# Strassen loop from token 1536, attention at every place of the plain blocks, spectral mixing with one step less

## The chip, the cores and the metric

The kernel runs on one core of a Trainium2 chip. The metric is the time of one execution on the device in microseconds (us), the median of several runs. The engines are called PE (TensorE, the matrix multiplier) with its weight loads (PEld), DVE (VectorE), ACT (ScalarE), POOL (GpSimd) and SP (SyncE, which issues nearly all DMAs here). Each engine executes its own instructions in order and waits for the others by semaphores.

## What is computed

Pooled attention, then two token and channel mixers in a row, on 8 batches of 576 tokens with 512 channels:

```python
# attention: 8 heads of 64; keys and values are means over 8 tokens (72 of them)
scores = scale * np.matmul(q, k_p.transpose(0, 1, 3, 2))
attn = softmax(scores);  x = attn @ v_p            # -> (8, 576, 512)
# first mixer
h = x.transpose(0, 2, 1) @ U @ V                   # rank 32, along the tokens
u = x + h.transpose(0, 2, 1)
x1 = u + np.maximum(u @ w_ch1, 0.0) @ w_ch2        # 512 -> 2048 -> 512
# second mixer
u = x1 + real(fft(fft(x1, axis=1), axis=2))        # spectral mixing
un = layernorm(u)
out = u + np.maximum(un @ w_ch1b, 0.0) @ w_ch2b
```

Numbers are 32 bits wide. The kernel splits a factor into a high and a low part where it needs the precision, so one product becomes three matmuls (high x high, high x low, low x high).

## The kernel before

The 4608 tokens go through the first mixer's channel layers in two ways. The **plain loop** takes the first `2 * SB` pieces of 256 tokens: first pieces 0 and 1 together (g0 below), then one piece at a time (the narrow blocks, g1 and on). A piece has 16 places `f`; at each stands 12 matmuls of 256 columns (`h<-utx,w`) and six of 512 columns (`o<-w,hh`, `o<-w,hl`). Its input is turned by DVE (`block_prep`). The **Strassen loop** takes all further work in blocks of 512 tokens: the rest of the first mixer, then all nine blocks of the second (k0 and on). A block has eight rounds; a round has seven products of six matmuls of 256 columns (`h<-x,wr`) with 24 matmuls of 512 columns between them. Its input is turned by PE: 16 transposes a block (`h<-ident,ul`, or `s<-ident,ul` in the second mixer). Its combined weights come from DRAM (`wc`) through a ring of four tiles (`wr`), 512 KB each, 28 in a block.

Beside these loops run **lanes**, Python generators that are advanced step by step: `a` (attention of a batch, tile by tile), `prep` (means of keys and values), `mix` (the rank 32 mixing), `p` (input of the next block), `w` (weights: `w_combine` makes the Strassen weights of the first mixer from the loaded ones, then `w_second` loads words of `w1b`, converts and combines them and stores them in `wc`, then quarter by quarter `w2b` into `wd`), and `d` (the spectral mixing of a batch, class `Dft`, with its loads `F` and `R` of `x1d` and their sum `S`). `w_combine` has 48 steps, the words of `w1b` 104 and the quarters of `w2b` 66. Weights in work lie in `wo`, a tile with four buffers.

In the plain loop a lane steps once at each place `f`, the weight lane twice at three places of four. In the Strassen loop a function `tick(i)` is called four times in a round with a row of lane names for each `i`; the attention lane steps a fifth time in a round. The lane `d` starts when all others but `p` are done. Batches from `LB` on use another form of the attention step: their rank 32 sum goes through bank `s1` and is added on DVE (`hus`), so that they can run in either loop.

Who sets the order: in the Strassen loop the instructions of PE, DVE and ACT stand as written; in the plain loop ACT's do from g1 on, while a scheduler places those of PE and DVE; on SP and POOL it places them everywhere. SP's queue is in order too: an issue that waits holds all issues behind it.

The places of the program that the change touches: the constants `SB` and `LB` (the first lines of the diff), `Dft.run` (its `yield`s, each of which ends a step), the condition ahead of `step("a")` in the plain loop, and the first row of names in `tick`.

Of the kernel before, what the change touches and what calls it, by code (L numbers as in the profile page):

```python
# [34 lines left out]
NPR = NF // 2  # L35
TA = 512
NBA = NTOK // TA
SB = 4
LB = 6
NOP = 12  # L40
NRING = 4
QAHEAD = 2
# [4 lines left out]
def kernel(  # L47
# [31 lines left out]
    state = {"n": 0, "free": False, "m": "s1", "u": 0, "slot": 0, "x1": 0, "u2": 0, "op": 0, "clock": 0, "flush": False, "lean": False, "four": False, "busy": False, "late": None, "tick": 0, "banks": ("s0", "s1", "hu")}  # L79
# [534 lines left out]
    class Dft:  # L614
# [18 lines left out]
        def run(self, b, group):  # L633
            p1 = self.p
            z = b * S
            slot = b - group[0]
# [26 lines left out]
            yield  # L663
            yield
            yield
            yield
            X, XE = [], []
            for i in range(3):
                f, r, n = fr
                s = tl("S")  # L670
                e = tl("E")
                add(nc.vector, s[:n], f[:n], r[:n])
                yield
                sub(nc.vector, r[:n], f[:n], r[:n])
                nc.gpsimd.tensor_copy(e[:n, 0:1], s[:n, 0:1])
                nc.gpsimd.memset(e[:n, 511:512], 0.0)
                sub(nc.vector, e[:n, 256:511], r[:n, 1:256], r[:n, 256:511])
                add(nc.vector, e[:n, 1:256], s[:n, 1:256], s[:n, 256:511])
                c2 = s[:n, 511:512].to_broadcast([n, 64])
                if i < 2:  # L680
                    fr = loads(i + 1)
                yield
                xe = tl(f"xe{i}", (128, 96 if i < 2 else 64), F32R)
                if i < 2:
                    xh, xl = tl(f"xh{i}", dt=F32R), tl(f"xl{i}", dt=F32R)
                    split(xh, xl, e)
                    nc.scalar.activation(out=xe[:, 0:64], in_=c2, func=ACTF.Copy)
                    sub(nc.vector, xe[:, 64:96], c2[:, 0:32], xe[:, 0:32].bitcast(F32))
                    X.append((xh, xl))
                    XE.append(xe)  # L690
                else:
                    m = self.sm
                    for h, y, w in ((xe, c2, 64), (None, e, 512)):
                        h = h or tl("S", dt=F32R)
                        q = r[:, 0:w]
                        nc.vector.tensor_scalar(out=q[:n], in0=y[:n], scalar1=m[:n, 0:1], scalar2=None, op0=ALU.mult)  # L696
                        nc.scalar.activation(out=h[:n], in_=y[:n], func=ACTF.Copy)  # L697
                        nc.vector.scalar_tensor_tensor(out=h[:n], in0=h[:n].bitcast(F32), scalar=m[:n, 1:2], in1=q[:n], op0=ALU.mult, op1=ALU.add)  # L698
                    X.append((h,))
                    XE.append(xe)  # L700
                yield
                if i < 2:
                    yield
                    yield
            P = []
            if slot == 0:
# [51 lines left out]
            for i in range(n2):  # L758
# [11 lines left out]
                a, bb = bank("s0"), bank("s1")  # L770
# [80 lines left out]
    pools = [mp]  # L851
    seq = [(0, b) for b in range(SB, NBA)] + [(1, b) for b in range(NBA)]

# [373 lines left out]

    groups = [[0, 1]] + [[j] for j in range(2, 2 * SB)]
    late = []
    slot = 0  # L1230
    order = ExitStack()
    for gi, js in enumerate(groups):
        if gi == 1:
            order.enter_context(tc.manual_schedule(engines={mybir.EngineType.Activation}))
        wide = len(js) > 1
        last = js[-1] == 2 * SB - 1
        tags = (("o0", "o1"), ("h1", "m"))
        for f in range(NF):
            state["slot"] = NF * gi + f
            clock()  # L1240
            while (1, min(f + 2, NF - 1)) not in W:
                step("w")
            one = wide or late or f % 2 == 0
            hs = st1(js, f, "h0" if one else "h1")
            if last and f >= NOP:
                ring_load(f - NOP)
            if late and f == 4:
                finish(late.pop())
                state["m"] = "m"
            if f == 0:  # L1250
                begun, rested = False, False
            if not begun and f >= (6 if gi == 1 or last else 1):
                if last:
                    ok = lambda: state["u"] >= (SB + 1) * TA
                else:
                    nj = groups[gi + 1][0]
                    ok = lambda: state["u"] >= (nj + 1) * T
                if f >= (NF - 1 if wide else 9):
                    until(ok)
                if ok():  # L1260
                    begun = True
                    lanes["p"] = prep_a(0) if last else block_prep(nj)
            if not df:
                if gi and "w" not in lanes and len(second) < 2:
                    lanes["w"] = (w_combine, w_second)[len(second)](at)
                    second.append(1)
                spectral()
            prev = hq.pop(0) if len(hq) >= (2 if gi > 1 or (gi == 1 and f > 0) else 1) else None
            for i in range(2 if wide else 1):
                slot += 1  # L1270
                if wide or slot % 4 or state["four"] or gi > 4:
                    step("a")
                step("d")
                if prev and i < len(prev[0]):
                    st2(prev[0][i], prev[1], prev[2][i], tags[i])
                for name in ("p", "mix", "w", "prep", "w") if f % 4 else ("p", "mix", "w", "prep"):
                    step(name)
                if last:
                    step("p")
                    step("p")  # L1280
            if prev and not wide and len(prev[0]) > 1:
                st2(prev[0][1], prev[1], prev[2][1], tags[1])
            if prev and prev[1] == NF - 1:
                finish(prev[0][0])
                if len(prev[0]) > 1:
                    late.append(prev[0][1])
                    rest(prev[0][1])
                else:
                    later(lambda j=prev[0][0]: state.update(x1=(j + 1) * T))
            hq.append((js, f, hs))  # L1290
            if f == NF - 1:
                until(lambda: "p" not in lanes, ["p"] if last else None)
            if not rested and f > 11 and begun and "p" not in lanes:
                rested = True
                rest(js[0])
# [5 lines left out]
    clock()  # L1301
    state["x1"] = SB * TA
    state["banks"] = ("s0",)
# [19 lines left out]
    def tick(i):  # L1323
        state["tick"] = i
        clock()
        swap()
        spectral()
        for name in (("d", "p", "a", "mix", "w"), ("d", "p", "a", "w", "mix", "w"), ("d", "p", "a", "prep", "mix", "w"), ("d", "a", "mix", "p"))[i]:
            step(name)

    def ready_for(k):
# [171 lines left out]
```

## Time and profile before

| | |
|---|---|
| median of 3 runs | 1903.48 us (1902.91 to 1907.74) |
| the profiled execution | 1906.44 us, span of its instructions 1904.6 us |
| PE, PEld busy | 1823.2 us (96%), 1635.6 us (86%) |
| DVE, ACT, POOL busy | 1067.6 us (56%), 717.0 us (38%), 194.3 us (10%) |
| mean granted clock of PE | 0.987 of full speed |
| DMA | 423.78 MB, mean 222 GB/s |
| plain loop, both pieces together (g0) | 71.9 to 201.1 us of the span |
| plain loop, six narrow blocks (g1 to g6) | 201.1 to 582.4 us |
| Strassen loop, 14 blocks (k0 to k13) | 582.4 to 1904.6 us |

Busy time is the union of an engine's instructions; the end of a matmul is modelled, so a small hole between matmuls can be covered. How long work on PE takes is therefore read better from the distance between the starts of consecutive matmuls. The stage limits are the starts of the first matmul of g0, of g1 and of k0. In rows of waits, `A <- B` means that engine A stood idle until B's result came.

### The profile page before, as it was taken

How to read it: one execution, taken by the hardware profiler on the slowest of the kernel's cores; microseconds unless marked ns; L12 is line 12 of the kernel's file. 1: busy time of each engine (PE TensorE's matmuls, PEld its weight loads, DVE VectorE, ACT ScalarE, POOL GpSimd, SP SyncE). 2: the span in 40 equal slices, each digit the busy share in tenths (PEclk: the TensorE clock that was granted, in tenths of full speed). 3: DMA queues.
4: the chain of work that ended last, by engine and by line, in shares of the span. 5: the costliest groups of instructions: out<-in, count | busy, mean ns of one | idle time of the engine just before them, and what ended most of it. 6: DMA issues, size and time to landing. Idle time of an engine off the chain costs nothing. (4 is left out here: it accounts for less than half of the span.)

```text
span 1904.6 us, 31941 instructions
## 1 busy us (share of the span) xinstructions
PE 1823.2 (96%) x11500; PEld 1635.6 (86%) x11500; DVE 1067.6 (56%) x2445; ACT 717.0 (38%) x2198; POOL 194.3 (10%) x340
## 2 busy tenths in 40 slices
PE   5689899999999999999999999999999999999999
PEld 4569788888888888899889898989998999999998
DVE  7894475656565665545465746564656544444332
ACT  5552444444454543333233432333333323233221
POOL 3340131212210000000000000000000000000000
PEclk9799999999999999999999999999999999999999
DMA  9653465857478787867677857685768575756564
GB/s 359 226 186 119 140 198 165 254 175 242 155 249 292 254 280 264 279 211 263 205 246 242 300 185 236 209 278 190 244 214 261 191 234 190 227 182 228 187 206 133
DMA packets 262974, 423.78 MB, mean 222 GB/s; under 512 B 45536, under 2 KB 72256, under 8 KB 262816
## 3 DMA queue, kind: packets, MB, share of 16 engines
q1 hardware_dynamic: 261888, 418.33, 67.2%
q0 software_dynamic: 928, 3.40, 0.5%
q8 instruction: 91, 1.49, 0.3%
q14 instruction: 67, 0.55, 0.1%
HBM read 342.09 MB, written 79.56 MB: 221 GB/s over the span
## 5 line engine op out<-in xcount | busy, mean ns | idle before, releaser
L119 PE MATMUL h<-x,wr 128*128 128x256 f32 x4704 | 642.4, 284 | 6.3 <-DMA wr<-wc 2.8
L119 PEld LDWEIGHTS h<-x,wr 128*128 128x128 f32 x4704 | 616.6, 191 | 37.0 <-DVE side L112 4.1
L119 PE MATMUL o<-w,hh 128*128 128x512 f32 x1312 | 371.4, 399 | 2.9 <-ACT hh L1036 1.6
L119 PEld LDWEIGHTS o<-w,hh 128*128 128x128 f32 x1312 | 229.3, 190 | 39.1 <-ACT hh L1036 4.8
L119 PE MATMUL h<-utx,w 128*128 128x256 f32 x1536 | 214.8, 288 | 17.4 <-DVE hl L1037 10.0
L119 PEld LDWEIGHTS h<-utx,w 128*128 128x128 f32 x1536 | 202.4, 193 | 30.4 <-DVE hl L1037 14.7
L119 PE MATMUL o<-w,hl 128*128 128x512 f32 x656 | 213.7, 396 | 2.3 <-DVE hl L1037 2.3
L112 DVE TENSOR_TENSOR side<-h,side 128x256 f32<-128x256 f32 x224 | 123.9, 553 | 153.4 <-PE h L119 152.6
L1314 ACT ACTIVATE hh<-side 128x256 fp32r<-128x256 f32 x224 | 116.8, 522 | 137.1 <-DVE side L112 129.9
L1314 ACT ACTIVATE hh<-h 128x256 fp32r<-128x256 f32 x112 | 43.1, 385 | 301.3 <-PE h L119 299.6
L1320 DVE SCALAR_TENSOR_TENSOR hl<-h,hh 128x256 fp32r<-128x256 f32 x112 | 47.4, 424 | 186.9 <-ACT hh L1314 186.9
L119 PEld LDWEIGHTS o<-w,hl 128*128 128x128 f32 x656 | 120.2, 189 | 25.2 <-DVE hl L1037 2.9
L1320 DVE SCALAR_TENSOR_TENSOR hl<-side,hh 128x256 fp32r<-128x256 f32 x224 | 123.4, 551 | 28.6 <-ACT hh L1314 28.5
L119 PE MATMUL m<-w,hh 128*128 128x512 f32 x464 | 127.8, 395 | 0.0
L119 PE MATMUL hu<-w,hh 128*128 128x512 f32 x448 | 122.2, 394 | 0.0
L510 ACT ACTIVATE s<-s,mx 128x72 f32<-128x72 f32 x296 | 90.2, 329 | 50.0 <-DVE mx L503 48.9
L109 POOL TENSOR_TENSOR wo<-wo 128x256 fp32r<-128x256 f32 x88 | 67.6, 784 | 302.6 <-ACT wo L115 253.2
L109 DVE TENSOR_TENSOR x<-ul,x 128x256 fp32r<-128x256 f32 x182 | 70.1, 421 | 41.8 <-ACT x L115 41.6
L119 PEld LDWEIGHTS m<-w,hh 128*128 128x128 f32 x464 | 80.4, 190 | 10.8
L119 PEld LDWEIGHTS hu<-w,hh 128*128 128x128 f32 x448 | 77.0, 190 | 10.1
L1361 ACT ACTIVATE side<-h 128x256 f32<-128x256 f32 x112 | 42.8, 382 | 107.3 <-PE h L119 107.2
L119 PE MATMUL m<-w,hl 128*128 128x512 f32 x232 | 72.6, 391 | 0.0
(253 smaller groups left out, 2362.5 us busy)
## 6 DMA issues: line engine op xcount, KB each, us to landing
wr<-wc SPq DMA_DIRECT2D x392, 512.0 KB
wc<-wo SPq DMA_DIRECT2D x88, 256.0 KB
x<-x SPq DMA_DIRECT2D x56, 256.0 KB
ur<-ud SPq DMA_DIRECT2D x36, 256.0 KB
x1d<-ur SPq DMA_DIRECT2D x36, 256.0 KB
ul<-u2d SPq DMA_DIRECT2D x36, 256.0 KB
ur<-u2d SPq DMA_DIRECT2D x36, 256.0 KB
out<-ur SPq DMA_DIRECT2D x36, 256.0 KB
```

Of the source, the lines that this page charges most:

```text
L109: eng.tensor_tensor(out=o, in0=a, in1=b, op=ALU.subtract)
L112: eng.tensor_tensor(out=o, in0=a, in1=b, op=ALU.add)
L119: nc.tensor.matmul(o, a, b, start=start, stop=stop, skip_group_check=True)
L510: nc.scalar.activation(out=s[:n, a], in_=v[:, k], func=ACTF.Exp, bias=mx[:n, a:a + 1], accum_out=sm[:n, a:a + 1])
L1314: nc.scalar.activation(out=hh[:, i], in_=c, func=ACTF.Relu)
L1320: nc.vector.scalar_tensor_tensor(out=hl[:, i], in0=c, scalar=0.0, in1=hh[:, i].bitcast(F32), op0=ALU.max, op1=ALU.subtract)
L1361: nc.scalar.activation(out=sb, in_=v, func=ACTF.Copy)
```

## The change

`SB` falls from 4 to 3: the plain loop ends at token 1536 instead of 2048, with pieces 0 and 1 and four narrow blocks, and the Strassen loop has 15 blocks, six of the first mixer. `LB` falls from 6 to 5. In the plain loop the attention lane now steps at each place of every narrow block; before, it left out every fourth place in blocks 1 to 4. The weight lane steps twice in `tick(0)` of the Strassen loop instead of once. In `Dft.run` two `yield`s go: one between a batch's first loads and their use, and one between the second or third loads and theirs.

```diff
-SB = 4
-LB = 6
+SB = 3
+LB = 5
...
             fr = loads(0)
             yield
             yield
             yield
-            yield
             X, XE = [], []
             for i in range(3):
                 f, r, n = fr
...
                 yield
                 if i < 2:
-                    yield
                     yield
...
             for i in range(2 if wide else 1):
                 slot += 1
-                if wide or slot % 4 or state["four"] or gi > 4:
+                if wide or slot % 4 or state["four"] or gi:
                     step("a")
                 step("d")
...
-        for name in (("d", "p", "a", "mix", "w"), ("d", "p", "a", "w", "mix", "w"), ("d", "p", "a", "prep", "mix", "w"), ("d", "a", "mix", "p"))[i]:
+        for name in (("d", "p", "a", "w", "mix", "w"), ("d", "p", "a", "w", "mix", "w"), ("d", "p", "a", "prep", "mix", "w"), ("d", "a", "mix", "p"))[i]:
             step(name)
```

The order of instructions shows what moves. Three places follow; `hst`, `xh`, `xl` and `ust` belong to the rank 32 mixing, `v,e` to attention times V, `wr` and `x_...` to a Strassen product.

On PE, a tile of attention of batch 6 stands before in the last narrow block, between the matmuls of the plain loop:

```order
L119 MATMUL o_5687<-w,hh 128x512 x2
L119 MATMUL o_5691<-w,hh 128x512 x2
L119 MATMUL s_6310<-xh,ust 128x512
L119 MATMUL s_6310<-xl,ust 128x512
L119 MATMUL h_6339<-utx,w 128x256 x11
L119 MATMUL s_6314<-v,e 128x128
L119 MATMUL s_6314<-v,e 128x192 x3
L119 MATMUL s_6314<-v,e 128x64
L119 MATMUL h_6339<-utx,w 128x256
```

Now all five tiles of this batch stand behind the start of the Strassen loop; on PE one of them reads:

```order
L119 MATMUL h_5099<-x_4659,wr 128x256 x6
L119 MATMUL hu<-w,hh 128x512 x4
L119 MATMUL hu<-w,hl 128x512 x2
L119 MATMUL s_5957<-xh,ust 128x512
L119 MATMUL s_5957<-xl,ust 128x512
L119 MATMUL s_5961<-v,e 128x128
L119 MATMUL s_5961<-v,e 128x192 x3
L119 MATMUL s_5961<-v,e 128x64
L119 MATMUL h_5934<-x_4866,wr 128x256 x6
```

The tile's matmuls are the same; they moved from between plain matmuls to between a round's products. Behind the start of the Strassen loop there are 12 tiles' attention times V where there were eight.

On DVE, the words of `w1b` (L150, L155 and L156 convert one word) stand before in the plain loop, between the `hl<-h` of its places:

```order
L503 TENSOR_REDUCE mx<-s_5732 128x4
L109 TENSOR_TENSOR wo<-wo 128x256
L150 TENSOR_SCALAR wo<-cv 128x256
L418 TENSOR_REDUCE kp<-raw 128x72
L155 SCALAR_TENSOR_TENSOR wo<-cv,wo 128x256
L1037 SCALAR_TENSOR_TENSOR hl<-h_5714,hh 128x256
```

The last 11 of the 32 words now stand in the Strassen loop, between its sums (`side`) and `hl`:

```order
L156 SCALAR_TENSOR_TENSOR wo<-cv,wo 128x256
L109 TENSOR_TENSOR wo<-wo 128x256
L112 TENSOR_TENSOR hus<-s_5326,hus 128x512
L150 TENSOR_SCALAR wo<-cv 128x256
L155 SCALAR_TENSOR_TENSOR wo<-cv,wo 128x256
L156 SCALAR_TENSOR_TENSOR wo<-cv,wo 128x256
L112 TENSOR_TENSOR side<-h_5099,side 128x256
L109 TENSOR_TENSOR hst<-hus,hst 32x512
```

Behind them moved all 32 quarters of `w2b`, of which 24 stood in the Strassen loop before.

On DVE in the spectral mixing, the sum `S<-F,R` of a batch's tail (99 rows) stands before behind two `hl` rounds after the splits `xl`, `xe` of the part ahead of it:

```order
L109 TENSOR_TENSOR xl_9717<-E,xh_9716 128x512
L109 TENSOR_TENSOR xe_9715<-S,xe_9715 128x32
L112 TENSOR_TENSOR side<-h_6400,side 128x256
L112 TENSOR_TENSOR ur<-o_8823,ur 128x512
L1320 SCALAR_TENSOR_TENSOR hl<-h_6400,hh 128x256
L1320 SCALAR_TENSOR_TENSOR hl<-side,hh 128x256
L112 TENSOR_TENSOR side<-h_9645,side 128x512
L112 TENSOR_TENSOR ur<-o_8851,ur 128x512
L1320 SCALAR_TENSOR_TENSOR hl<-side,hh 128x512
L112 TENSOR_TENSOR S<-F,R 99x512
```

Now, on DVE at the same place, it comes after one `side`:

```order
L109 TENSOR_TENSOR xl_9831<-E,xh_9830 128x512
L109 TENSOR_TENSOR xe_9829<-S,xe_9829 128x32
L109 TENSOR_TENSOR x_9836<-ul,x_9836 128x2x128
L109 TENSOR_TENSOR x_9839<-ul,x_9839 128x2x128
L112 TENSOR_TENSOR side<-h_5099,side 128x256
L112 TENSOR_TENSOR S<-F,R 99x512
```

The sum moved ahead of three `hl` rows and a `side`, a step closer to the loads of `F` and `R`, which are issued where the part ahead of it is summed.

## Rows read from the trace of the kernel before

**Rows 1.** Windows by stage: start and end, length, busy PE, PEld, DVE, ACT, POOL, clock, DMA.

```profile
core 0 of [0], span 1904.6 us
...
201.10:582.40 381.30, 362.60 (x2307) 323.58 (x2308) 234.66 (x549) 172.75 (x675) 77.33 (x108) 0.99 0.64 201
582.40:785.50 203.10, 197.84 (x1254) 177.82 (x1253) 115.86 (x270) 86.84 (x292) 5.14 (x12) 0.99 0.83 280
```

**Rows 2.** Timeline of PE in a clean Strassen stretch: start, length, instruction.

```profile
1247.27 1.59 PE L119 MATMUL h<-x,wr 128*128 128x256 f32 x12
1248.71 1.09 PE L119 MATMUL m<-w,hh 128*128 128x512 f32 x4
...
1250.09 1.59 PE L119 MATMUL h<-x,wr 128*128 128x256 f32 x12
```

**Rows 3.** The same timeline in the first Strassen block, with attention.

```profile
600.10 1.14 PE L119 MATMUL s<-k,q 128*128 128x144 f32 x8
600.99 1.69 PE L119 MATMUL h<-x,wr 128*128 128x256 f32 x12
...
610.27 1.53 PE L119 MATMUL s<-v,e 128*128 128x128 f32 x10
611.60 1.68 PE L119 MATMUL h<-x,wr 128*128 128x256 f32 x12
...
620.61 0.66 PE L933 MATMUL h<-ident,ul 128*128 128x128 f32 x4
621.02 0.96 PE L119 MATMUL h<-x,wr 128*128 128x256 f32 x6
```

**Rows 4.** PE's groups in 201.1 to 582.4 us: count, busy, mean ns, idle before.

```profile
L119 PE MATMUL h<-utx,w 128*128 128x256 f32 x1152 | 164.0, 287 | 11.3 <-DVE hl L1037 10.0 <-ACT utx L115 1.0
L119 PE MATMUL o<-w,hh 128*128 128x512 f32 x380 | 115.2, 404 | 2.5 <-ACT hh L1036 1.2 <-DVE ur L112 0.6 <-ACT wo L115 0.6
L119 PE MATMUL o<-w,hl 128*128 128x512 f32 x190 | 68.6, 405 | 0.0
L119 PE MATMUL s<-v,e 128*128 128x192 f32 (+2 forms) x220 | 34.1, 300 | 0.0
L119 PE MATMUL s<-k,q 128*128 128x144 f32 x176 | 29.3, 292 | 0.6 <-DVE x L539 0.5
L516 PE MATMUL s<-ident,s 128*128 128x128 f32 x88 | 18.8, 280 | 3.0 <-ACT s L510 3.0
```

**Rows 5.** DVE's waits in 201.1 to 582.4 us: total us, times, longest.

```profile
DVE wo L109 <- DMA wc<-wo: 14.8, 14, 1.9
...
DVE cv L150 <- DMA wo<-w2b: 6.8, 4, 4.7
...
DVE wo L150 <- DMA cv<-w1b: 3.3, 2, 1.7
```

**Rows 6.** DVE's waits in 582.4 to 785.5 us, the first row.

```profile
DVE hl L1320 <- ACT hh L1314: 36.0, 21, 2.8
```

**Rows 7.** PE's waits in 582.4 to 785.5 us, the first row.

```profile
PE h L119 <- DMA wr<-wc: 2.0, 1, 2.0
```

**Rows 8.** Timelines of SP, DVE and PE at the first, fourth, fifth and last tail.

```profile
803.78 0.27 SPq L656 DMA_DIRECT2D R<-x1d  x1
...
806.92 0.68 DVE L112 TENSOR_TENSOR S<-F,R 99x512 f32<-99x512 f32 x1
...
1091.80 0.40 PE L119 MATMUL s<-st,S 99*128 99x290 f32 x1 [1.16 <-DVE S L698]
...
1184.73 0.21 SPq L656 DMA_DIRECT2D R<-x1d  x1
...
1186.39 0.69 DVE L112 TENSOR_TENSOR S<-F,R 99x512 f32<-99x512 f32 x1 [0.83 <-DMA R<-x1d]
...
1453.40 0.27 SPq L656 DMA_DIRECT2D R<-x1d  x1
...
1461.63 0.68 DVE L112 TENSOR_TENSOR S<-F,R 99x512 f32<-99x512 f32 x1
```

## The prediction

> **What bounds the kernel now.** I read the windows by stage first. The span is 1904.6 us. The first two Strassen blocks hold TensorE busy for 197.8 of 203.1 us, the six narrow plain blocks for 362.6 of 381.3 us [rows 1]. So TensorE's own work sets the time, and what can be won beside it lies in the holes of the plain stage, which are twice as dense (4.9% against 2.6%). Busy time hides part of those holes, because a matmul's end is modelled, so I counted the work itself.
>
> The second view is the timeline of TensorE in a clean Strassen stretch: twelve matmuls of 256 columns take 1.44 us (1247.27 to 1248.71), 0.120 us each, and six of 512 columns take 1.38 us (to 1250.09), 0.230 us each [rows 2]. The third is the same view where attention runs: eight score matmuls 0.89 us, ten of attention times V 1.33 us, four transposes 0.41 us [rows 3]. The fourth is the table of TensorE's groups in the six narrow plain blocks, which gives the counts [rows 4]. Their work is 1152 x 0.120 = 138.2; 634 matmuls of 512 columns (380 and 190 in the rows, and 64 in rows left out: two for each of 22 attention tiles and 20 of the mixing) x 0.230 = 145.8; 220 x 0.133 = 29.3; 176 x 0.111 = 19.6; 125 transposes (88 in the row, 37 left out) x 0.1025 = 12.8. That is 345.7 us of work in 381.3 us: **35.6 us lost, 5.9 us in each narrow block**, nearly twice the idle time of 18.7 us that the window shows.
>
> The fifth view says who is late: the waits of VectorE in that stretch. Nine of its rows name a DMA, 79.7 us in all; most of it is `wo` tiles that wait for their stores (40.8 us in three of the nine), and one wait of 4.7 us is for a `w2b` load [rows 5]. VectorE executes in order, so `hl` stands behind such a wait, and TensorE waits for `hl` (10.0 us on the first group of [rows 4]). In the first two Strassen blocks, where attention and the weight lane run too, the longest row of the same view is `hl` waiting for ScalarE, and none of its ten rows names a DMA [rows 6]. There TensorE is idle 5.3 of 203.1 us [rows 1]; by the plain stage's ratio (35.6 to 18.7) I call that 10 us lost.
>
> **The change part by part.**
>
> *One block of 512 tokens goes from the plain loop to the Strassen loop.* Two narrow blocks issue 2 x 16 x 12 = 384 matmuls of 256 columns; a Strassen block issues 8 x 7 x 6 = 336; the 192 of 512 columns stay. So 48 x 0.120 = 5.76 us of TensorE go. But the plain blocks turn their input on VectorE, a Strassen block on TensorE: 16 transposes x 0.1025 = 1.64 us come. Together **-4.1 us**, and this part stands on the path, since TensorE is the bound before and after. One block more of weights from DRAM (28 ring loads of 512 KB) lies beside it: the first two Strassen blocks ran at a DMA share of 0.83 [rows 1].
>
> *Four narrow blocks stay of six.* At 5.9 us each they lose 23.7 us in place of 35.6. Against that, attention now steps at each of 16 places in a block, where blocks 1 to 4 of before skipped every fourth, so its waits come closer together; I take 26 us. Bounds: 10 us (four blocks at the rate of the first two Strassen blocks, 10 us for 1024 tokens) and 35.6 us (nothing gained). **-9.6 us.**
>
> *What moves into the Strassen loop.* By the order, 12 attention tiles stand behind its start where 8 stood, all 32 quarter loads of `w2b` where 24 stood, and 11 words of `w1b` where there was none. The weight lane steps five times in a product round, not four. Three blocks carry lanes, not two. The longest wait of TensorE in those two blocks is 2.0 us for a weight ring load [rows 7], 3.8 us by the same ratio, and comes once. The other 6.2 us are at most 3.1 us for a further block and at least nothing; I take 1.1, since a part of them belongs to the entry into the loop, which comes once as well. The moved words bring their `wo` waits along: the plain blocks of after take 4 x 28 of the 152 steps that use `wo` so, 40 are left, and 40/152 of 40.8 us are 11 us of VectorE waits. At the plain stage's exchange (35.6 of 79.7) they cost 4.8 us, and nothing if the Strassen order covers them: between the sum that frees a half bank and the next product in it lie one product and six matmuls, 0.72 + 1.38 = 2.1 us [rows 2]. I take half, 2.4. **+3.5 us**, bounds 1 and 6.
>
> *Spectral mixing with a step less.* A step is a quarter of a round of 7 products and 24 matmuls of 512 columns, (5.04 + 5.52)/4 = 2.64 us. Loads of `F` and `R` are used a step sooner. From the issue of the last load of a batch's tail to its sum on VectorE there were 2.9, 2.8, 1.9, 3.7, 1.5, 8.0, 3.8 and 8.0 us in the eight batches (first, fifth and last in [rows 8]). In the fifth VectorE waited 0.83 us, so a load takes 2.28 us from issue to use. With 2.64 us less, six of the eight come late, by 2.1, 2.2, 3.0, 1.2, 3.5 and 1.2 us, 13.1 us of VectorE waits. The Trainium skill, "DMA: Bandwidth & Descriptors", section "Anatomy of one DMA", speaks against this edit: a DMA has a fixed cost of about 2 us, most of it the receipt of the last byte, whatever its size. [...] What reaches TensorE is less: each wait has the 2.1 us of cover above, and the tail's matmul stands three steps behind. I take **+2 us**, bounds 0 and 13.1.
>
> **Sum.** -4.1 - 9.6 + 3.5 + 2.0 = -8.2 us: a span of 1896.4 us. The profiled run took 1906.44 us, 2.96 above the median of 1903.48 us; against the median it is 1903.48 - 8.2 = **1895.3 us**. This kernel's runs can tell about 0.3%, 5.7 us, from no change, so faster means under 1897.8 and slower over 1909.2.
>
> **The rivals.** (A) The forecast, 1890 to 1900 us.
>
> (B) The holes move with the lanes. They come from weight steps and loads, and these are all still done; then the second and third part cancel, and 1903.5 - 4.1 + 2.0 = 1901.4 us. For it: the `wo` waits are half of VectorE's DMA waits and follow the weight lane. Against it: no DMA wait at all on VectorE in the first two Strassen blocks.
>
> (C) Slower: the spectral sums wait for their loads. If TensorE paid the whole step at each of eight tails, 8 x 2.64 = 21.1 in place of 2.0, the time would be 1903.5 - 10.2 + 21.1 = 1914.4 us. For it: the tail's matmul already waited 1.16 us for VectorE in the fourth batch [rows 8], so some chains have no slack. It decides from 2.0 us per batch ((10.2 + 5.7)/8). Against it: five of the eight tails would come at most 2.1 us late, which the cover takes.
>
> (D) More is won: the remaining plain blocks lose half of what they did, 2.95 us each, since the `w2b` wait and a part of the `wo` waits are no longer theirs, and the Strassen loop covers what it takes over: 11.8 - 35.6 = -23.8, and 1903.5 - 4.1 - 23.8 + 1 = 1876.6 us; half way from A, 1886 us.
>
> That the change does nothing can't be: the order shows the block moved.
>
> **How the numbers follow.** A 0.56, B 0.23, C 0.12, D 0.09. A lies under 1897.8 for seven parts in ten (0.40); D is faster whole; of B a tenth is, and the rest is the same; C is slower. So faster 0.52, same 0.36, slower 0.12. The range 1885 to 1906 holds A, B and a part of D and leaves out C.
>
> **What would show it.** Right: the narrow blocks (now four) still take 60 to 65 us each; the blocks with lanes in the Strassen loop, now three, have few VectorE rows that name a DMA; 5040 matmuls of 256 columns on the ring where there were 4704, and 1152 on `utx`; in the spectral stretch VectorE rows S waiting for R of 1 to 3 us at some tails, with TensorE idle under 1 us there. Wrong: TensorE idle in the first three Strassen blocks of over 10 us with the ring or `hl` as the releaser, narrow blocks over 68 us, or a spectral stretch with several idle microseconds a batch.

## The result, and the profile after

The changed kernel takes **1927.82 us** (median of 4 runs, 1926.81 to 1929.37), the kernel before 1904.85 us on the same chip (4 runs, 1902.91 to 1907.74): a ratio of 1.012, interval 1.0103 to 1.0138. It is 23 us slower, where 8.2 us less were forecast. The profiled execution took 1927.33 us with a span of 1925.5 us, 20.9 us longer than before.

The counts came out as forecast. Two groups of the page's table (busy time, mean ns, idle before):

```profile
L119 PE MATMUL h<-x,wr 128*128 128x256 f32 x5040 | 692.1, 285 | 18.5 <-DVE side L112 10.4
L119 PE MATMUL h<-utx,w 128*128 128x256 f32 x1152 | 156.8, 287 | 10.0 <-DVE utx L109 3.9
```

So the time went into waits. The windows, cut as in [rows 1] (the four narrow blocks one by one, then k0, k1, k2, k3 to k9, the rest):

```profile
199.80:268.80 69.00, 63.19 (x399) 54.96 (x399) 39.31 (x90) 29.92 (x124) 14.97 (x21) 1.00 0.57 179
268.80:337.50 68.70, 64.94 (x409) 56.68 (x408) 42.35 (x96) 29.51 (x123) 16.10 (x22) 1.00 0.56 175
337.50:406.90 69.40, 65.57 (x411) 56.85 (x410) 40.38 (x94) 30.51 (x130) 14.03 (x19) 1.00 0.65 204
406.90:467.00 60.10, 59.42 (x394) 54.09 (x393) 46.79 (x114) 35.73 (x137) 12.11 (x16) 1.00 0.80 266
...
467.00:596.20 129.20, 113.68 (x701) 101.81 (x700) 75.94 (x170) 62.58 (x223) 19.83 (x29) 0.95 0.80 267
596.20:695.50 99.30, 97.36 (x612) 86.62 (x610) 60.84 (x145) 44.57 (x146) 3.85 (x7) 1.00 0.88 301
695.50:794.10 98.60, 97.35 (x614) 87.33 (x614) 56.62 (x132) 39.25 (x121) 0.00 (x0) 1.00 0.78 259
794.10:1485.10 691.00, 676.49 (x4321) 612.35 (x4320) 389.68 (x929) 232.10 (x586) 45.22 (x145) 0.99 0.72 234
1485.10:1925.50 440.40, 436.69 (x2742) 393.38 (x2740) 184.04 (x437) 126.57 (x316) 10.28 (x16) 1.00 0.64 202
```

One block stands out: k0, 129.2 us long, TensorE busy for 113.7 of them at a granted clock of 0.95. No other block is near it.

As in the prediction I count what a block **loses**: its length less its matmuls at their prices from start to start, here instruction by instruction. In k0 the products and their 512-column matmuls make 80.5 us, attention 22.5, mixing and transposes 2.9, together 105.9, so it loses 23.4 us (with the block limits unrounded). By this count the six narrow blocks of before lost 32.9 us (35.6 by the group prices of the prediction). All losses below are counted so, each from one profiled execution.

| lost, us | before | after |
|---|---|---|
| narrow blocks | 32.9 (six) | 26.3 (four: 9.7, 7.7, 7.8, 1.2) |
| Strassen blocks with attention and weights | 9.2 (k0 4.5, k1 4.7) | 29.8 (k0 23.4, k1 4.1, k2 2.3) |
| spectral blocks | 8.7 (k2 to k9) | 21.2 (k3 to k9) |

The differences, -6.6 + 20.6 + 12.5, with -4.1 of work and 1.3 us that the time up to g1 became shorter, make +21.1 us; the spans differ by 20.9.

Who is late in k0: the waits of DVE and then of PE in 467.0 to 596.2 us (total, times, longest).

```profile
DVE wo L150 <- DMA wc<-wo: 13.6, 3, 5.1
...
DVE wo L109 <- DMA wc<-wo: 2.1, 2, 1.6
```

```profile
PE h L514 <- DVE hl L1318: 6.5, 2, 4.9
PE h L119 <- DVE side L112: 5.1, 2, 4.7
```

15.7 us of waits for stores of `wo`, in five waits. Before, the plain stage had them in short pieces: 14 with the longest 1.9 us in [rows 5], and in the two rows left out there at most 2.5 and 3.2 us. One of the three long ones, on SP, DVE and PE (`SPq` is the issue of a DMA):

```profile
478.30 0.32 SPq L136 DMA_DIRECT2D wc<-wo  x1
478.89 0.32 SPq L1070 DMA_DIRECT2D ur<-ud  x1
479.61 0.98 SPq L136 DMA_DIRECT2D wc<-wo  x2
```

```profile
478.43 0.41 DVE L112 TENSOR_TENSOR side<-h,side 128x256 f32<-128x256 f32 x1
483.87 0.29 DVE L150 TENSOR_SCALAR wo<-cv 128x256 int32<-128x256 int32 x1 [5.03 <-DMA wc<-wo]
484.97 0.42 DVE L1318 SCALAR_TENSOR_TENSOR hl<-h,hh 128x256 fp32r<-128x256 f32 x1 [0.81 <-ACT hh L1312]
```

```profile
478.89 1.69 PE L119 MATMUL h<-x,wr 128*128 128x256 f32 x12 [0.41 <-DVE side L112]
485.45 0.42 PE L514 MATMUL h<-ident,s 128*64 128x128 f32 x1 [4.88 <-DVE hl L1318]
```

SP issues three stores within 2.3 us. The next word (L150) needs one of the four `wo` tiles back and stands 5.03 us; `hl` stands behind it on DVE, and PE waits 4.88 us for `hl`. That is not the end of it. The windows of PE around this hole:

```profile
480.30:485.30 5.00, 0.28 (x3) 0.07 (x1) 0.62 (x2) 1.00 (x3) 0.00 (x0) 0.91 1.03 377
485.30:486.50 1.20, 1.05 (x5) 0.99 (x6) 1.17 (x5) 0.36 (x2) 0.00 (x0) 0.50 1.06 408
...
490.00:491.00 1.00, 1.00 (x4) 0.81 (x3) 0.38 (x2) 0.00 (x0) 0.00 (x0) 0.50 0.70 225
491.00:492.00 1.00, 1.00 (x6) 0.81 (x6) 0.09 (x1) 0.00 (x0) 0.00 (x0) 0.88 0.94 352
...
595.00:596.00 1.00, 1.00 (x4) 0.81 (x3) 0.00 (x0) 0.35 (x1) 0.00 (x0) 0.50 0.90 78
```

Behind the hole the granted clock is 0.50 (1.2 GHz, the lower of the two levels) from 485.3 to 491 us, and PE is busy at it: 5.7 us of matmuls that would take half of that. A hole of 4.9 us costs about 7.7. The second, at 585.8 us, is a wait of 4.7 us with the same half clock behind it. The two together make about 15 of the 23.4 us that k0 loses. In the first hole the DMA share is 1.03, against 0.80 in the whole block: the stores run while the DMA engines are full. The Trainium skill, "TensorE: Matmul & The Clock Gate", Part 1, says that the throttled level is the default and activity releases it; the rows agree.

In the spectral stretch (794.1 to 1485.1 us) DVE's sums wait for loads, where there was one wait of 0.83 us before [rows 8]. The row, and the longest of the six, on SP, DVE and PE:

```profile
DVE S L112 <- DMA R<-x1d: 17.0, 6, 8.3
```

```profile
1409.57 1.09 SPq L647 DMA_DIRECT2D R<-x1d  x3
1410.77 2.97 SPq L979 DMA_DIRECT2D wr<-wc  x2
```

```profile
1417.01 0.69 DVE L112 TENSOR_TENSOR S<-F,R 128x512 f32<-128x512 f32 x1 [8.30 <-DMA R<-x1d]
```

```profile
1418.76 2.20 PE L119 MATMUL h<-x,wr 128*128 128x256 f32 x12 [3.33 <-DVE side L112]
```

This is not a tail but the first sum of the last batch: its loads are issued by 1410.66 us, two ring loads of `wr` come right behind them, and the sum starts 6.35 us after the last issue. `side` stands behind it on DVE; PE waits 3.33 us.

The longest hole of the stretch is another one, in k3, the first block with spectral mixing. On PE, and its windows:

```profile
813.56 2.90 PE L119 MATMUL h<-x,wr 128*128 128x256 f32 x12 [3.79 <-DMA wr<-wc]
```

```profile
816.00:818.00 2.00, 2.00 (x8) 1.61 (x7) 0.41 (x2) 0.00 (x0) 0.10 (x1) 0.50 1.05 393
```

PE waits 3.79 us for a weight ring load, and half clock follows to about 819 us. Together that is the 6 us or so that k3 loses; PE has no other wait in k3.

### The profile page after: what moved, and what is told of

Read it like the earlier page. It is cut to its first block, busy times and chain, and to the rows that moved or that the text cites. A ratio compares the mean times of both kernels' runs of the same rounds, so it can differ in the third digit from the quotient of the medians.

```text
span 1925.5 us, 32019 instructions
## 1 busy us (share of the span) xinstructions
PE 1826.9 (95%) x11468; PEld 1633.4 (85%) x11468; DVE 1082.4 (56%) x2471; ACT 729.9 (38%) x2229; POOL 196.3 (10%) x340
## 5 line engine op out<-in xcount | busy, mean ns | idle before, releaser
L119 PE MATMUL h<-x,wr 128*128 128x256 f32 x5040 | 692.1, 285 | 18.5 <-DVE side L112 10.4
L119 PEld LDWEIGHTS h<-x,wr 128*128 128x128 f32 x5040 | 661.4, 192 | 52.6 <-DVE side L112 13.6
L119 PE MATMUL o<-w,hh 128*128 128x512 f32 x1248 | 348.8, 399 | 4.4 <-ACT hh L1034 4.1
L119 PEld LDWEIGHTS o<-w,hh 128*128 128x128 f32 x1248 | 217.6, 191 | 38.8 <-ACT hh L1034 8.5
L119 PE MATMUL o<-w,hl 128*128 128x512 f32 x624 | 199.2, 396 | 2.2 <-DVE hl L1035 2.2
L119 PE MATMUL h<-utx,w 128*128 128x256 f32 x1152 | 156.8, 287 | 10.0 <-DVE utx L109 3.9
L119 PEld LDWEIGHTS h<-utx,w 128*128 128x128 f32 x1152 | 148.2, 192 | 18.2 <-DVE hl L1035 6.5
L1318 DVE SCALAR_TENSOR_TENSOR hl<-side,hh 128x256 fp32r<-128x256 f32 x240 | 132.7, 553 | 31.2 <-ACT hh L1312 31.2
L119 PE MATMUL m<-w,hh 128*128 128x512 f32 x496 | 136.5, 395 | 0.0
L119 PE MATMUL hu<-w,hh 128*128 128x512 f32 x480 | 131.7, 396 | 0.0
```

The costliest lines, as they stand in the source:

```text
L119: nc.tensor.matmul(o, a, b, start=start, stop=stop, skip_group_check=True)
L1318: nc.vector.scalar_tensor_tensor(out=hl[:, i], in0=c, scalar=0.0, in1=hh[:, i].bitcast(F32), op0=ALU.max, op1=ALU.subtract)
```

## The experiments

Each was timed in three rounds beside the kernel before, whose medians were 1902.9, 1905.4, 1905.3, 1904.9 and 1904.9 us in the five sets. Theory 1, made from the two traces: the words of `w1b`, closer together by the fifth weight step, make k0's loss, and the spectral sums' wait for their loads makes most of that of k3 to k9, independently. Theory 2: the spectral blocks lose because three blocks of lanes run ahead of and beside them, not through the step. The rival for k0: the attention tiles that moved there cost it, not the words.

### First set: which part costs

**Spectral steps alone**, on the kernel before:

```diff
             fr = loads(0)
...
-            yield
...
                 if i < 2:
-                    yield
                     yield
```

> The kernel before with the spectral mixing's missing steps alone. Theory 1 (two prices add up: words of w1b that moved into the Strassen loop cost about 19 us in its first block, and spectral sums that wait for their loads cost about 12 us): 8 to 13 us slower than before, lost in the blocks with spectral mixing. Theory 2 (the spectral blocks lose because of the lanes moved beside them, not because of the step): within 3 us of before.

1914.43 us, ratio 1.0055 (1.0035 to 1.0075): 11.5 us over the kernel before, as theory 1 says. Waits of S for R rose to 13.9 us in seven. The profiled execution was the fastest of the four (1908.87 us), so its blocks can't say where the 11.5 us lie.

**Spectral steps put back**, on the changed kernel (the same lines with +):

> The changed kernel with the spectral mixing's steps restored. Theory 1: 10 to 13 us faster than the changed kernel, about 1916 us, with the sums S not waiting for R; the first Strassen block still loses over 20 us. Theory 2: 1926 to 1929 us.

1922.93 us, 1.0101 (1.0075 to 1.0128): 5 us less than the changed kernel, half of the 10 to 13 expected, and not the 11.5 that the step took alone. S still waits for R, 8.9 us in five. k0 still loses 22.6 us.

**One weight step in `tick(0)`**, on the changed kernel:

```diff
-        for name in (("d", "p", "a", "w", "mix", "w"), ("d", "p", "a", "w", "mix", "w"), ("d", "p", "a", "prep", "mix", "w"), ("d", "a", "mix", "p"))[i]:
+        for name in (("d", "p", "a", "mix", "w"), ("d", "p", "a", "w", "mix", "w"), ("d", "p", "a", "prep", "mix", "w"), ("d", "a", "mix", "p"))[i]:
```

> The changed kernel with one weight step in tick 0 as before, so the words come further apart in the Strassen loop. Theory 1: the waits for free wo tiles get shorter, the first Strassen block loses some 10 us less, about 1918 us. Rival A (the moved attention tiles cost it, not the words): attention is the same, 1926 to 1929 us.

1915.24 us, 1.0054 (1.0037 to 1.007). k0 loses 9.4 us instead of 23.4. Its window and DVE's wait for stores in it:

```profile
466.60:581.90 115.30, 111.00 (x701) 99.01 (x700) 70.75 (x160) 59.30 (x214) 16.13 (x24) 0.99 0.83 276
```

```profile
DVE wo L150 <- DMA wc<-wo: 8.0, 2, 4.1
```

Of the 13 words that begin in k0 by time 11 still do, and the longest wait is only 1 us shorter; but PE is idle 4.3 us in all, with no hole over 1.5 us, and the clock is 0.99. So a wait's length alone does not set its price. That the price is the part of it over the cover fits both runs, but no run shows it by itself.

**One more weight step at each plain place**, on the changed kernel, so that all words are done in the plain loop:

```diff
-                for name in ("p", "mix", "w", "prep", "w") if f % 4 else ("p", "mix", "w", "prep"):
+                for name in ("p", "mix", "w", "w", "prep", "w") if f % 4 else ("p", "mix", "w", "prep", "w"):
```

> The changed kernel with one more weight step at each place of the narrow blocks, so that all words of w1b end in the plain loop and 13 quarters of w2b too; attention tiles stand as in the changed kernel. Theory 1: the first Strassen block loses 5 to 8 us in place of 23, the narrow blocks 3 to 8 us more: 1915 to 1920 us. Rival A: the first Strassen block still loses about 20 us and the plain loop loses more, 1930 us or over.

1953.88 us, 1.0259 (1.024 to 1.0277). k0 loses 8.8 us without a word in it, a little over the 5 to 8 expected; but the four narrow blocks lose 73.7 us instead of 26.3, far over the 3 to 8 us more of theory 1. The time is the rival's, its reason (k0 still loses 20 us) is not. VectorE's waits for stores of `wo` do not explain it: in the narrow blocks they are 36.0 us, and 36.4 in the changed kernel. What rose is PE's waits for ScalarE (this run, then the changed kernel, each in its four narrow blocks):

```profile
PE o L119 <- ACT hh L1034: 21.0, 22, 3.0
```

```profile
PE o L119 <- ACT hh L1034: 3.7, 8, 1.4
```

What holds ScalarE up there, no run tells apart.

### Second set: the words in k0

**Both taken back** (spectral steps and weight step):

> The changed kernel with the spectral steps and the fifth weight step both taken back: what stays is the Strassen loop from token 1536 and attention at every place. Theory 1 (two separate losses, the words of w1b in k0 and the spectral loads): the gains of the two taken back singly, 12.6 and 4.9 us by their medians, add up: 1907 to 1913 us, k0 loses 8 to 11 us, k3 to k10 together under 16. Theory 2 (lanes beside the spectral blocks cost them anyway): the same time as with the weight step alone taken back, 1914 to 1918 us.

1917.8 us, 1.0065 (1.0048 to 1.0082): the two gains do not add up; beside the weight step alone taken back (1915.24 us) the spectral steps win nothing. k0 loses 8.4 us, but k5, the block ahead of the second mixer, 12.4. It lost some 12 with the weight step alone taken back, too, so this is a price of that step and does not say why the spectral steps win nothing beside it. PE there:

```profile
1050.56 0.30 PE L119 MATMUL s<-st,S 99*128 99x290 f32 x1
1052.02 0.54 PE L119 MATMUL s<-st,xh 128*128 128x290 f32 x2 [1.16 <-DVE pl L109]
...
1054.22 0.53 PE L119 MATMUL s<-st,xh 128*128 128x290 f32 x2 [1.00 <-DVE pl L109]
```

Spectral stages stand one behind the other with no product between them: `until`, which steps `d` and `p` until the next block's input is ready. The first pair of batches must be done before the block ahead of the second mixer (k4 before, k5 now); the weight lane at four steps a round ends later, so the spectral lane starts later. This is theory 3, which I had not thought of.

**Words slower** (a step more in each, in the Strassen loop alone), on the changed kernel:

```diff
             high(raw, 256, t)
             yield
+            if state["lean"]:
+                yield
             bits(raw, 256, t)
```

> The changed kernel, weight steps as changed (five in a round), but each word of w1b takes one step more while the Strassen loop runs, so that its stores come about as far apart as with four steps. Theory 1 (the stores of the words set the loss, not the number of weight steps): k0 loses 9 to 13 us instead of 23.4, 1913 to 1919 us. Rival (the fifth weight step in a round is itself too much for VectorE's place in front of hl): k0 still loses 20 us or more, 1925 to 1930 us.

1920.92 us, 1.0082 (1.0066 to 1.0097). k0 loses 14.2 us with five weight steps a round, but the words now reach into k1, which loses 7.9 (4.1 in the changed kernel): between the two theories, nearer the first.

**Stores of the words issued by POOL**, on the changed kernel:

```diff
-            store(wc[1][n], o.bitcast(F32).rearrange("p h x -> p (h x)"))
+            later(lambda: nc.gpsimd.dma_start(out=wc[1][n], in_=o.bitcast(F32).rearrange("p h x -> p (h x)")))
```

> The changed kernel with the stores of the words of w1b issued by POOL behind its own subtraction and not by SP. If the late issue on SP's queue makes the wait of wo, the waits of VectorE for wo stores in k0 fall from 13.6 us to under 6 and k0 loses 10 to 15 us: 1912 to 1920 us. If the way of the store to DRAM beside the ring loads makes it, the waits stay at 10 us or more and the time at 1923 to 1930 us.

1930.49 us, 1.0131 (1.0114 to 1.0147). The issues come at 477.1 us, 1.2 us earlier, but the word still starts at 483.45. The DMA view of k0 (count, KB, median us from issue to landing) and the two timelines:

```profile
wc<-wo POOLq DMA_DIRECT2D x25, 256.0 KB, 4.8
```

```profile
477.14 1.63 POOL L263 DMA_DIRECT2D wc<-wo  x3
```

```profile
483.45 0.29 DVE L150 TENSOR_SCALAR wo<-cv 128x256 int32<-128x256 int32 x1 [5.64 <-DMA wc<-wo]
```

Moving the issue off SP's queue wins nothing: issued earlier, the tile comes back at nearly the same time, 6.3 us after the first issue, with a DMA share of 1.00 from 478.0 to 483.5 us. In k0 a store of 256 KB took 4.8 us from POOL's queue at a mean share of 0.77. That speaks for the way of the store; but the trace has no landing of stores from SP's queue, so that they take as long is inferred. By the Trainium skill, "DMA: Bandwidth & Descriptors", "Anatomy of one DMA", a fixed 2.0 us and 436 GB/s make 2.6 us, an estimate for a DMA by itself; beside the ring loads the row has nearly twice that, and the row decides.

**The fifth weight step alone**, on the kernel before (the `tick` line the other way):

> The kernel before with the fifth weight step in a round alone. No word of w1b stands in its Strassen loop, only 24 quarters of w2b. Theory 1: no more than 3 us either way, 1900 to 1906 us, k0 and k1 lose 8 to 12 us together as before. Rival (the step itself costs): k0 loses 10 us or more instead of 4.5, 1908 us or more.

1909.4 us, 1.0017 (1.0004 to 1.0029), 10 runs. k0 and k1 lose 12.9 us together instead of 9.2. The step without words costs 3 to 4 us, a little over what theory 1 allows and far from the rival.

### Third set: late lanes, and attention without pauses

**Fifth weight step for the quarters alone**, on the changed kernel, with the spectral steps as changed and then with them **put back**:

```diff
         ahead = [load2(i) for i in range(3)]
+        state["quarters"] = True
...
             step(name)
+        if i == 0 and "quarters" in state:
+            step("w")
```

(and one `"w"` in the row of `tick(0)`)

> The changed kernel with the fifth weight step in a round only once the words of w1b are done, so for the quarters of w2b alone. Theory 1 (holes in k0 come from words too close together): k0 loses 8 to 11 us as with the step taken back. Theory 3 (new: with the step taken back altogether the spectral lane starts too late, and the block ahead of the second mixer has to push it without spacing): k5 loses under 6 us where it lost 12, since the quarters end earlier: 1909 to 1915 us. Against theory 3: k5 still loses 10 us or more, 1916 us or more.

> The same with the two spectral steps put back. If the spectral sums' wait for their loads is a loss of its own, 4 to 8 us less than the run beside it, 1904 to 1911 us, k3 to k10 lose under 14 us together. If the longer batches then miss the second mixer's start, k5 loses 8 us or more and the time stays at 1912 us or more.

1919.35 us, 1.0074 (1.0059 to 1.0089), and 1913.65 us, 1.0044 (1.0029 to 1.0059). The first is a miss: k5 falls to 5.8 us as theory 3 says, but k1 to k4 lose 18.5 us where they lost 8.1 with the step taken back, so the lane's earlier end wins nothing by itself. The second is the best form of the changed kernel, 5.7 us under the first, but over the 1904 to 1911 forecast. The S waits of the first and then of the second:

```profile
DVE S L112 <- DMA R<-x1d: 17.2, 6, 6.7
```

```profile
DVE S L112 <- DMA R<-x1d: 7.1, 5, 3.4
```

**Spectral lane three rounds later**, on the kernel before:

```diff
     def lane_d(df):
+        for _ in range(12):
+            yield
```

> The kernel before with 12 idle steps (three rounds) ahead of the first spectral batch and nothing else. Theory 3: the first pair of batches is done three rounds into the block ahead of the second mixer (k4), its preparation is pushed without spacing, k4 loses 8 us or more instead of 0.3: 1911 to 1919 us. Rival (the lane has slack there): k4 under 3 us, 1900 to 1907 us.

1912.11 us, 1.0031 (1.0017 to 1.0045), 10 runs; k4 loses 5.8 us instead of 0.3 in a profiled run that was the fastest of the ten. Theory 3 has the sign and the place; the block's loss is under the 8 us forecast.

**Attention at every place alone**, on the kernel before:

```diff
-                if wide or slot % 4 or state["four"] or gi > 4:
+                if wide or slot % 4 or state["four"] or gi:
```

> The kernel before with attention at every place of the narrow blocks and nothing else. By the prediction's second part the holes follow the lanes' work, so g1 to g4 lose more (22 to 28 us instead of 17.2) and g5 and g6 less: 1901 to 1909 us. Rival (closer steps cost more in all): the six lose 40 us or more and the time is over 1910 us.

1919.27 us, 1.0067 (1.0048 to 1.0087): the rival. The six narrow blocks lose 40.4 us instead of 32.9, and k0 and k1, which have less attention now, 14.2 instead of 9.2.

### Fourth set: the tiles, and the pauses put back

**A fifth `wo` tile** in the Strassen loop, made room for by six tiles of input instead of seven, and the **control** with the six alone, both on the changed kernel:

```diff
-        return pools[-1].tile([128, DM], F32, tag="u", name=name, bufs=2 if len(pools) == 1 else 7)
+        return pools[-1].tile([128, DM], F32, tag="u", name=name, bufs=2 if len(pools) == 1 else 6)
...
         def wo(self):
+            if state["lean"]:
+                state["wo"] = state.get("wo", 0) + 1
+                if state["wo"] % 5 == 0:
+                    return pools[-1].tile([128, 2, 256], F32R, tag="wo2", name="wo")
```

> The changed kernel with a fifth tile for weights in work (wo) in the Strassen loop, and six instead of seven tiles for the input there to make room. If the holes of k0 are VectorE waiting for a wo tile whose store is still on its way, a tile more gives each store about one step (2.6 us) more: the waits for wo stores in k0 fall from 13.6 us to under 6, none is over 3.5 us, k0 loses 8 to 15 us instead of 23.4, and the time is 8 to 15 us under the control beside it. If the fifth step costs in another way: no more than 3 us under the control.

> Control for the fifth wo tile: the changed kernel with six instead of seven tiles for the input of the blocks in the Strassen loop and nothing else. 1925 to 1936 us: no gain, and at most 8 us of new waits for an input tile.

1921.19 us and 1931.65 us. The fifth tile wins 10.5 us; k0 loses 15.7 us against 26.0. The windows of k0, fifth tile and control:

```profile
471.90:593.40 121.50, 110.66 (x702) 99.46 (x700) 75.02 (x169) 62.10 (x221) 19.48 (x29) 0.97 0.83 274
```

```profile
470.30:602.20 131.90, 115.64 (x701) 103.89 (x701) 76.29 (x170) 62.77 (x223) 19.98 (x29) 0.93 0.79 260
```

The long waits fall from three to two (9.3 us against 14.5), less than expected (under 6 us in all, none over 3.5): one of 6.0 us is left. The control shows no gain from six tiles of input.

**Pauses put back** in the first three narrow blocks, on the best form above:

```diff
-                if wide or slot % 4 or state["four"] or gi:
+                if wide or slot % 4 or state["four"] or gi > 3:
```

> The kernel with quarters alone at the fifth step and the spectral steps put back (1913.65 us), and with attention's pauses put back in the first three of the four narrow blocks; of the change only the loop's start at token 1536 and attention without pauses in the last narrow block stay. If attention without pauses costs by itself (14 us in the kernel before): g1 to g3 lose 12 to 18 us instead of 28, 1903 to 1910 us. If the work that it leaves comes back as loss in k0 to k2 (more than 25 us there instead of 17): 1911 to 1917 us.

1941.89 us, 1.0197 (1.0175 to 1.0219), worse than both forecasts. g1 to g3 lose 14.2 us as expected, but g4 11.7, k1 and k2 19.6 with attention that came late, and k3 21.3 and k5 9.6 with spectral stages pushed. So with this order of the lanes the loop's start at token 1536 needs attention without pauses.

### Fifth set: wider steps in the kernel before

**Pauses in the fifth narrow block too** (`gi > 5` in place of `gi > 4`), and **in all six** (that condition left out):

> The kernel before with attention's pauses in the fifth narrow block too. If a block's loss follows the closeness of the steps: g5 loses 2 to 4 us instead of 7.5, and four attention steps more behind the start of the Strassen loop, under one round: 1899 to 1904 us. If attention then comes late for k0 and is pushed in g6: g6 loses 12 us or more, 1906 us or more.

> The kernel before with attention's pauses in all six narrow blocks, but for the batches from 6 on, which have none in either. Wider steps alone: g5 and g6 lose 6 us instead of 15.8, 1896 to 1903 us. Late lanes: attention is pushed at the end of g6 or the spectral lane starts later, 1907 us or more.

1897.4 us, 0.9964 (0.995 to 0.9978), and 1899.29 us, 0.9968 (0.9952 to 0.9985). With the pauses in the fifth block it loses 2.2 us, as forecast; with pauses in all six, g5 and g6 still lose some 10.5 together, not 6.

**Second weight step at every other place**, with the fifth step a round for quarters alone:

```diff
-                for name in ("p", "mix", "w", "prep", "w") if f % 4 else ("p", "mix", "w", "prep"):
+                for name in ("p", "mix", "w", "prep", "w") if f % 2 else ("p", "mix", "w", "prep"):
```

> The kernel before with the second weight step at every other place instead of three places of four, and a fifth step a round for the quarters of w2b alone: 24 steps, some eight words, move into the Strassen loop at four steps a round. If the narrow blocks' loss follows the closeness of the weight steps: the six lose 20 to 26 us instead of 33, k0 loses 8 to 10 instead of 4.5, the spectral lane starts two to three rounds later (the late spectral lane cost 6 us): 1900 to 1908 us. If the plain loss doesn't follow it: 1911 us or more.

1898.15 us, 0.9965 (0.9952 to 0.9978). All three beat both kernels, by 0.3 to 0.4% of the kernel before. The windows of the narrow blocks, pauses in the fifth, then the wider weight steps (and its k0):

```profile
201.20:569.90 368.70, 354.44 (x2283) 317.36 (x2284) 230.84 (x542) 170.32 (x656) 76.73 (x108) 1.00 0.66 207
```

```profile
200.10:565.50 365.40, 356.67 (x2304) 320.80 (x2305) 222.76 (x518) 167.10 (x659) 72.65 (x101) 1.00 0.63 196
565.50:684.50 119.00, 109.10 (x696) 98.39 (x695) 67.96 (x161) 58.42 (x222) 7.37 (x12) 0.97 0.77 262
```

Against 381.3 us in [rows 1]. The six lose 23.4 and 17.6 us instead of 32.9; of the latter k0 gives back 9.9 (it loses 14.4, where 8 to 10 were forecast). Only two words begin in it; one long wait makes most of the loss. DVE and then PE in this k0:

```profile
DVE wo L109 <- DMA wc<-wo: 8.3, 2, 7.8
```

```profile
PE h L515 <- DVE hl L1321: 6.9, 1, 6.9
```

So one hole can take back half of what the wider steps won.

## Why the prediction was wrong, point by point

**First part, the block's work (-4.1): right.** The counts are those forecast.

**Second part, four narrow blocks instead of six: 26 us lost forecast, 26.3 measured.** The closeness is in part luck, since the two are counted differently: by the prediction's own group prices the four lose about 28 us. The gain is 6.6 us, not 9.6, since the six of before lost 32.9 by the finer count. But I let attention without pauses cost 2.3 us (26 against 23.7). The three blocks that have it lose 7.7 to 9.7 us and take 69 us, not 60 to 65; the fourth, where little attention is left, loses 1.2. Alone, that edit cost the kernel before 14 us, and it can't be left out here (pauses put back: 1941.89 us).

**Third part, what moves into the Strassen loop: this is the step that failed.** I took +3.5 us with bounds of 1 and 6; it is +20.6. The amount of waits was nearly right: 11 us of VectorE waits forecast for the moved words, 15.7 us seen in k0. Their price was wrong. I took the plain stage's exchange (35.6 of 79.7) as the upper end and cover by 2.1 us as the lower. Both are averages over short waits. In k0 two waits of 5.03 and 5.11 us left TensorE idle for 4.88 and 4.70 us, nearly whole, and it then worked at half clock for about 6 us each time. The upper end should have been the whole waits and the clock behind them. Three runs bear on the cause: k0 without words loses 8.8 us; with 11 of its 13 words, at four steps a round, 9.4; with a fifth `wo` tile 15.7 against 26.0. Rival (B) had the direction, that holes move with the lanes, but at the plain stage's price; that no DMA wait stood in the first Strassen blocks [rows 6] spoke of blocks without words.

**Fourth part, spectral mixing (+2, bounds 0 and 13.1): mechanism right, size off.** By medians the step costs 5.7 us with the quarters alone at the fifth step (1919.35 to 1913.65), 4.9 in the changed kernel, 11.5 in the kernel before, and nothing beside the weight step taken back (1915.24 to 1917.8): there is no one price. Rival (C) named it. I misread the one tail that waited: its sum starts 1.45 us after the last issue, and the 0.83 us of waiting lie within that [rows 8]. So its load took 1.45 us, not 2.28, and the waits come to about 8.9 us, not 13.1. The fixed cost of about 2 us that the prediction takes from the Trainium skill, "DMA: Bandwidth & Descriptors", "Anatomy of one DMA", stands there for DMAs issued by GpSimd. This load, issued by SP, was used 1.66 us after the start of its issue, so the row does not bear that figure out. And I looked at tails alone: the largest wait, 8.3 us, is at a batch's first sum, with loads that took over 6 us while ring loads ran beside them. The 12.5 us more that the spectral blocks lose are not all the step's: some 6 of the 21.2 are k3's wait for a ring load, and it stays (3.9 us) with the spectral steps put back. The kernel before waits 2.0 us at the same place, the start of the spectral lane [rows 7].

**Not in the prediction: lanes that end late.** The first pair of spectral batches has to be done ahead of the second mixer, and attention ahead of its block; a lane that is late is pushed without spacing. So an edit that widens steps can pay at the next deadline (k5 with the weight step taken back, k3 and k5 with the pauses put back), and gains need not add.

**What would show it.** I had named narrow blocks over 68 us as a sign against me; three of the four came so. I had also named TensorE idle by over 10 us in the first three Strassen blocks with the ring or `hl` as the releaser. TensorE is idle for 18.7 us there, but only 7.4 have these releasers (6.5 and 0.9); another 6.9 have `side`, which at 585.8 us stood behind the same kind of wait.

**Open.** Even the best form with the loop at token 1536 is 8.4 us slower than the kernel before of its set. Its profile loses 29.4 us in the narrow blocks, 17.0 in k0 to k2 and 13.5 in the spectral blocks, 9.1 us more than before where 4.1 of work were saved; the 5.5 us of k3 in it are again a wait of 3.9 us for a ring load, with half clock behind it. Why that load comes late there, and not with four weight steps a round, stays open. So does what the lanes that end late cost the changed kernel itself, since its k5 loses only some 4 us. Single executions of one kernel spread by up to 11 us, so single profiles can't settle differences of a few us between blocks.

## What to carry to other kernels

Price a wait by its length in the place where it comes to stand, with the clock behind it, not by a share of the total: sort the waits by length before moving work. Steps of side work that share an in-order engine with the main loop want distance: with 24, 28 and 44 weight steps a narrow block lost 2.9, 5.5 and 18.4 us (the last beside attention without pauses, where 28 went with 6.6, and with ScalarE, not the stores, as what TensorE waited for). And look for the deadline of each lane before making it slower.

## What I had not expected of the hardware

A hole of 4.9 us on TensorE had 5.7 us at half the granted clock (1.2 GHz) behind it, so that it cost about 7.7. A 256 KB store to DRAM, issued by POOL, took 4.8 us in the median to land at a mean DMA share of 0.77. Issuing the stores there instead of on SP won nothing (1930.49 against 1927.82 us), while a fifth tile won 10.5 us.
